# Linear attention with an ELU feed-forward: three uncast first loads, one decayed k, and a written-out order

## The chip, the core and the metric

The kernel runs on one core of a Trainium2 chip. Five engines work side by side, each through its own list of instructions in order: TensorE (PE, matrix products, with its weight loads shown apart as PEld), VectorE (DVE), ScalarE (ACT), GpSimd (POOL) and SyncE (SP). Transfers run on 16 DMA engines. A transfer is issued by SP or ACT on a hardware queue, or by POOL on a software queue; in this kernel a load that turns 32-bit floats into 16-bit ones is issued by POOL. The metric is the device time of one execution in microseconds (us). A kernel's time is the median of several runs.

## The reference

The first part is attention without a softmax, with a decay `lam` per head, in blocks with a running state; the second is a feed-forward layer with ELU.

```python
B, H, S, D = q.shape                      # 4, 8, 768, 64; block = 64
Dmask = np.where(rel >= 0, lam[:, None, None] ** rel[None, :, :], 0.0)
lam_pow = lam[:, None, None] ** (pos[None, :, None] + 1)
for b in range(nb):
    intra = np.einsum('bhic,bhjc->bhij', qb, kb) * Dmask[None]
    intra = np.einsum('bhij,bhjd->bhid', intra, vb)
    inter = np.einsum('bhid,bhde->bhie', qb * lam_pow[None], kv_state)
    out[:, :, sl] = intra + inter
    rev_pow = lam[:, None, None] ** (block - 1 - pos[None, :, None])
    kb_dec = kb * rev_pow[None]
    kv_state = lam_block * kv_state + np.einsum('bhsd,bhse->bhde', kb_dec, vb)
# then, with x of 3072 tokens x 512:
h = x @ w_in                              # 512 x 2048
g = np.where(h > 0.0, h, np.exp(np.minimum(h, 0.0)) - 1.0)
return (g @ w_out).astype(np.float32)     # 2048 x 512
```

## The kernel before

**Tiles.** The kernel takes blocks of 128 positions, not 64, so a sequence has 6 chunks. A *group* g is one chunk of one batch: g // 4 is the chunk and g % 4 the batch, 24 groups in all. A group is 128 tokens by 512 features (8 heads of 64). Groups 0 to 3 are loaded one by one, later ones in pairs. `w_in` and `w_out` are loaded in eight pieces each (`wi16_0` to `7`, `wo16_0` to `7`). Tiles on the chip are 16-bit, the arrays in memory 32-bit.

**Work of a group.** `T`: q and k are transposed, on PE with an identity for groups 0 to 7 (into `psT`, line 283, copied out on DVE to `qT` with a multiply by `qs` in line 290 and on ACT to `kT` in line 291), by DMA transposes on SP's queue for later groups (line 268). `S`: products of k and q into two `psS` (302). `E`: DVE multiplies them by `mask`, which holds causality and a decay (318), into `pp`. `P`: `pp` and v into `psO` (338), and from chunk 1 on the state and q too (344). Then `psO` goes to `xt`, on ACT (359) or, from group 8, on DVE with a multiply by `qs` (361). `kd`: POOL multiplies k by its decay `ks` (174). `U`: kd and v into `psU` (397 as four matmuls, 406 as eight of half width), and DVE adds it to the old state, which POOL has multiplied by `upp` (378), giving the new state `st` (416, 418).

**Feed-forward.** `1:g:j`: 16 matmuls (8 of 256 columns once groups go in pairs) with pieces of wi into `psH` (478), which has two banks; ACT writes `e` = exp (484) and relu in place (485); DVE joins both to `g` (457), which frees the bank. `2:g:j`: four matmuls with pieces of wo into `psM` (499); after four such units the row of the output goes to `osb` (525) and out over SP (450). A unit `1:g:j` with j = 0 needs wi pieces 0 and 1 in groups 0 to 3, j = 1 pieces 2 and 3, and so on; the same holds for `2:g:j` and wo.

**Order.** Every engine works through its instructions as written. POOL's list is `POOL_ORDER` (k0 is a load, i0 a piece of wi, o0 of wo, d0 a multiply `kd`, m4 a state multiply). `OPEN` is the order of all other work up to the first unit of group 8, where w2 and w6 are matmuls on zeros; from there a loop at the end of the function writes the order with the offsets in `AT` and a lag `LAGU` of the `2` units. In front of everything stand ten matmuls on zeros (line 84). `q0` is the one tile that is loaded in 32 bits, on SP's queue (line 117), and cast on DVE (127). `BANKS` says which of the eight PSUM banks each result takes.

Some results of DVE and ACT (`pp`, `xt`, state updates) are kept in a list `late` and issued one at a time between feed-forward units.

Of the kernel before, what the change touches and what calls it, by code (L numbers as in the profile page):

```python
# [7 lines left out]
FP32 = mybir.dt.float32  # L8
# [7 lines left out]
def kernel(  # L16
# [30 lines left out]
    POOL_ORDER = (  # L47
        "k0 k1 iota q1 k2 v1 i0 v0 q2 i1 v2 i2 o0 i3 d0 q3 o1 i4 k3 i5 o2 o3 v3 d1 m4 d2 d3 i7 "
        "o4 o5 i6 o7 k4 o6 q4 m5 k6 v4 q6 k10 q10 d5 d4 d6 m6 v6 k8 q8 v8 d7 m7 v10"
    )  # L50
    RAW = "q0"
    FIRST = "q0:0 c0 c1 c2"
    OPEN = (
        "z1 z0 z3 Z1 Z2 Z0 z2 T0 w2 T1 S0 S1 w6 P0 P1 T2 1:0:0 S2 1:1:0 P2 U0 M 1:2:0 1:0:1 2:0:0 "
        "1:1:1 2:1:0 1:2:1 T3 2:2:0 1:0:2 S3 1:2:2 2:2:1 2:1:1 P3 1:1:2 1:3:0 2:0:1 2:0:2 "
        "2:1:2 1:1:3 U1 1:2:3 M Z3 2:2:2 1:3:2 U2 1:3:1 2:1:3 1:0:3 T5 T4 2:2:3 1:3:3 S4:5 "
        "2:0:3 2:3:2 2:3:0 M U3 M B:P4:P5:U4:U5 W8 2:3:3 1:4:1 T6 W9 1:4:0 T7 2:3:1 1:4:3 S6:7 "
        "1:4:2 2:4:0 2:5:0 1:4:5 1:4:4 2:4:1 B:P6:P7:U6:U7 1:4:7 1:6:1 2:5:2 2:5:1 1:6:0 1:4:6 "
        "2:4:2 S8:9 1:6:2 1:6:3 2:4:3 2:5:3 W11 W10 1:6:4 B:P8:P9:U8:U9 1:6:5 1:6:6 2:6:0 "
        "2:6:1 L12 1:6:7 2:6:2 1:8:0 S10:11 2:6:3 1:8:1 2:7:0 1:8:2 2:7:1"  # L60
    )
    LAGU = 7
    AT = {"L": -18, "W": -13, "T": -9, "S": -8, "B": -4}
    BANKS = (
        "S0=M0,M1 S1=C,D S2=D,M1 S3=D,B P0=M1 P1=B P2=B P3=D U0=M0 U1=D U2=A U3=M1 T0=M1,C "
        "T1=D,A T2=A,D T3=D T4=M0 T5=A T6=M1 T7=D M2=C M3=M0"
# [14 lines left out]
    def zero_matmuls(n):  # L81
# [4 lines left out]
    zero_matmuls(10)  # L86
# [4 lines left out]


# [27 lines left out]
    nc.scalar.preload_act_table_set("natural_log_exp_and_others")  # L120

    def cast_raw(g, w, eng):
        n = f"{w}{g}"
        t = asb.tile([128, 1, H, 64], FP16, tag=f"{w}n1", name=f"{w}n{g}", bufs=4)
        (qg if w == "q" else kg)[g] = t
        if eng == 0:
            nc.vector.tensor_copy(t[:, 0], raw[n][:])
        else:
            nc.scalar.copy(t[:, 0], raw[n][:])

    def of(tiles, g):
        g0, i = group_of[g]
        return tiles[g0][:, i]
# [25 lines left out]

    iota_c = cpool.tile([128, 1], I32, name="iota_c")  # L160
    iota_r = cpool.tile([128, 128], I32, name="iota_r")

    def emit_iota():
        nc.gpsimd.iota(iota_c[:], pattern=[[0, 1]], base=0, channel_multiplier=1)
        nc.gpsimd.iota(iota_r[:], pattern=[[1, 128]], base=0, channel_multiplier=0)

    kds, qkT, Pt, psS, xg = {}, {}, {}, {}, {}

    def att_kd(g):
        if g // B == NCB - 1:  # L170
            return
        kd = asb.tile([128, H, 64], FP16, tag="kd", name=f"kd{g}", bufs=8)
        kds[g] = kd
        nc.gpsimd.tensor_tensor(  # L174
            out=kd[:], in0=of(kg, g),
            in1=ks[:].unsqueeze(2).broadcast_to([128, H, 64]), op=ALU.mult,
        )


    pool_list = POOL_ORDER.split()  # L180

    def emit_pool():
        w = pool_list.pop(0)
        if w == "iota":
            emit_iota()
        elif w[0] in "qkv":
            emit_load(w[0], int(w[1:]))
        else:
            {"i": emit_wi, "o": emit_wo, "d": att_kd, "m": lambda g: att_M(g)}[w[0]](int(w[1:]))

    def emit_pool_run():
        while pool_list and pool_list[0][0] != "m":
            emit_pool()

# [15 lines left out]

    dn = cpool.tile([128, H], FP32, name="dn")
# [451 lines left out]
```

## Time and profile before

| | us |
|---|---|
| runs: median of 3 (lowest, highest) | 215.49 (215.18, 215.7) |
| the profiled execution: span from first to last instruction | 213.2 |
| TensorE busy | 202.7 |
| VectorE, ScalarE busy | 130.1, 129.0 |
| GpSimd busy | 96.2 |
| TensorE busy, 0 to 5 us | 3.81 |
| TensorE busy, 5 to 10 us | 2.95 |
| TensorE busy, 15 to 20 us | 3.88 |
| TensorE busy, 35 to 50 us | 15.0 of 15 |

The span is less than the time of a run; the difference of the median, 2.3 us, lies before the first and after the last instruction. Busy time of TensorE is counted from the start of a matmul to its modelled end; matmuls overlap, so that one of 512 columns lasts some 380 ns in the table but the next starts 216 ns after it. Work on TensorE is therefore counted here by the distance from start to start. The granted clock is 1.00 nearly throughout, though the first ten matmuls on zeros start 0.43 us apart.

A line of the order of time reads: start, duration, engine, line of the kernel, operation, result <- sources, count, and in brackets how long the engine was idle before and what ended that.

### The profile page before, as it was taken

To read this page: it belongs to the slowest core of one execution; us is meant where nothing else is said; L and a number is where in the kernel's file an instruction comes from. 1 tells how busy PE (TensorE), PEld (TensorE's weight loads), DVE (VectorE), ACT (ScalarE), POOL (GpSimd) and SP (SyncE) were. 2 spreads that over 40 slices of the span, in tenths; PEclk is the share of its full clock that TensorE was granted. 3 is DMA by queue.
4 is the path that set the end of the run, shared out by engine and by line. 5 is a ranking of instruction groups with operands and counts; after the bars stand their busy time and mean duration, and the time that the engine had idled before them with its cause. 6 is when DMAs were issued, how large, how long until landed. Compare 5 with 4: busy or idle time off the path is not lost.

```text
span 213.2 us, 5156 instructions
## 1 busy us (share of the span) xinstructions
PE 202.7 (95%) x2066; PEld 138.1 (65%) x2066; DVE 130.1 (61%) x224; ACT 129.0 (61%) x245; POOL 96.2 (45%) x115
## 2 busy tenths in 40 slices
PE   7667999999999999999999999999999999999994
PEld 2355676767686776766766766766766666666652
DVE  3936453777846888677667667667667547533321
ACT  4545654884867756676476476476476576477640
POOL 7996991999972908667166259300000000000000
PEclk9999999999999999999999999999999999999999
DMA  8999999999996999999939919999124110110112
GB/s 90 141 175 193 192 148 173 147 165 147 153 165 145 111 197 107 144 122 116 129 106 125 167 59 103 144 180 161 52 65 83 52 49 0 54 51 16 36 49 98
DMA packets 101976, 24.59 MB, mean 115 GB/s; under 512 B 92608, under 2 KB 99008, under 8 KB 101952
## 3 DMA queue, kind: packets, MB, share of 16 engines
q0 software_dynamic: 79760, 13.50, 83.1%
q1 hardware_dynamic: 22192, 10.76, 24.6%
q8 instruction: 16, 0.26, 0.5%
q14 instruction: 8, 0.07, 0.1%
HBM read 27.27 MB, written 6.29 MB: 157 GB/s over the span
## 4 chain that ended last, share of the span: by engine, by line
PE 82%; POOL 8%; DMA 7%; issue 1%; ACT 1%; DVE 0%; POOLq 0%; ACTq 0%
PE psM L499 36%; PE psH L478 35%; DMA wi<-in_moe_w_in_dram 4%; DMA wo<-in_moe_w_out_dram 3%; PE psO L338 3%; PE psS L302 3%; PE psO L344 2%; POOL kd L174 1%; POOL wi L148 1%; POOL kn L109 1%; POOL vn L109 1%; PE psU L406 1%; PE psT L283 1%; POOL qn L109 1%; POOL wo L155 1%
## 5 line engine op out<-in xcount | busy, mean ns | idle before, releaser
L478 PE MATMUL psH<-xt,wi 128*128 128x256 f16 (+1 forms) x896 | 99.3, 258 | 2.0 <-DMA wi<-in_moe_w_in_dram 1.1
L457 DVE SCALAR_TENSOR_TENSOR g<-e,psH 128x512 f16<-128x512 f32 x96 | 65.8, 686 | 56.7 <-ACT psH L485 56.0
L484 ACT ACTIVATE e<-psH 128x512 f32<-128x512 f32 x96 | 57.3, 597 | 65.0 <-PE psH L478 62.8
L499 PE MATMUL psM<-wo,g 128*128 128x512 f16 (+1 forms) x384 | 95.6, 377 | 0.7 <-DMA wo<-in_moe_w_out_dram 0.7
L478 PEld LDWEIGHTS <-wi 128*128 128x128 f16 x896 | 76.9, 98 | 27.4 <-DMA wi<-in_moe_w_in_dram 1.8
L485 ACT ACTIVATE psH<-psH 128x512 f32<-128x512 f32 x96 | 57.0, 593 | 0.0
L499 PEld LDWEIGHTS <-g 128*128 128x128 f16 x384 | 35.9, 98 | 29.3 <-issue 1.3
L318 DVE TENSOR_TENSOR pp<-psS,mask 128x512 f16<-128x512 f32 x48 | 30.8, 684 | 4.4 <-PE psS L302 4.4
L174 POOL TENSOR_TENSOR kd<-kn,ks 128x512 f16<-128x512 f16 x20 | 20.7, 1040 | 21.3 <-DMA kn<-in_k_dram 20.4
L378 POOL TENSOR_TENSOR stt<-st,upp 64x256 f32<-64x256 f16 x32 | 19.5, 608 | 14.7 <-DVE st L418 8.9
L109 POOL DMA_DIRECT2D vn<-in_v_dram x14 | 15.5, 1108 | 1.7 <-DMA wi<-in_moe_w_in_dram 1.7
L109 POOL DMA_DIRECT2D kn<-in_k_dram x14 | 15.5, 1105 | 0.8 <-POOLq L647 0.8
L525 ACT COPY osb<-psM 128x512 f32<-128x512 f32 x23 | 13.5, 590 | 3.2 <-PE psM L499 3.2
L109 POOL DMA_DIRECT2D qn<-in_q_dram x13 | 14.8, 1138 | 0.0
L418 DVE TENSOR_TENSOR st<-stt,psU 64x256 f16<-64x256 f32 x32 | 13.3, 416 | 1.2 <-PE psU L406 0.5
L361 DVE TENSOR_TENSOR xt<-psO,qs 128x512 f16<-128x512 f32 x16 | 11.0, 688 | 3.5 <-PE psO L344 3.5
L338 PE MATMUL psO<-pp,vn 128*64 128x128 f16 x192 | 12.0, 222 | 1.2 <-DMA vn<-in_v_dram 1.0
L338 PEld LDWEIGHTS <-vn 128*64 128x64 f16 x192 | 9.7, 110 | 4.6 <-issue 2.9
L344 PE MATMUL psO<-qT,st 128*64 128x128 f16 x160 | 10.0, 219 | 0.0
L344 PEld LDWEIGHTS <-st 128*64 128x64 f16 x160 | 8.9, 110 | 0.0
L302 PE MATMUL psS<-qT,kT 64*128 64x128 f16 x192 | 7.9, 218 | 0.3 <-ACT kT L291 0.3
L359 ACT CAST xt<-psO 128x512 f16<-128x512 f32 x8 | 4.4, 588 | 6.4 <-PE psO L338 4.3
(44 smaller groups left out, 72.3 us busy)
## 6 DMA issues: line engine op xcount, KB each, us to landing
out_dram<-osb SPq DMA_DIRECT2D x23, 256.0 KB, 2.2
kn<-in_k_dram POOLq DMA_DIRECT2D x10, 256.0 KB, 7.8
qn<-in_q_dram POOLq DMA_DIRECT2D x10, 256.0 KB, 6.8
vn<-in_v_dram POOLq DMA_DIRECT2D x10, 256.0 KB, 7.6
wi<-in_moe_w_in_dram POOLq DMA_DIRECT2D x8, 256.0 KB, 6.9
wo<-in_moe_w_out_dram POOLq DMA_DIRECT2D x8, 256.0 KB, 7.7
kn<-in_k_dram POOLq DMA_DIRECT2D x4, 128.0 KB, 4.2
vn<-in_v_dram POOLq DMA_DIRECT2D x4, 128.0 KB, 5.5
```

Of the source, the lines that this page charges most:

```text
L109: nc.gpsimd.dma_start(out=t[:].rearrange("p b h d -> p (b h) d"), in_=src)
L174: nc.gpsimd.tensor_tensor(out=kd[:], in0=of(kg, g), in1=ks[:].unsqueeze(2).broadcast_to([128, H, 64]), op=ALU.mult,)
L302: nc.tensor.matmul(psS[g][hh][:, hp, :], lhsT=kt[r, hp, :], rhs=qt[r, hp, :], start=True, stop=True,)
L318: nc.vector.tensor_tensor(out=P[:], in0=pts[hh][:], in1=mask[:, hh::2, :], op=ALU.mult)
L338: nc.tensor.matmul(po[r, hp, :], lhsT=vt[:, 2 * hp + hh, :], rhs=Pt[(g, hh)][:, hp, :], start=True, stop=(cb == 0), skip_group_check=True,)
L344: nc.tensor.matmul(po[r, hp, :], lhsT=st[b][cb % 2][:, hp, r], rhs=qt[:, hp, :], start=False, stop=True, skip_group_check=True,)
L378: nc.gpsimd.tensor_tensor(out=tmp[r], in0=old[r, :, r], in1=upp[r].unsqueeze(2).broadcast_to([64, NHP, 64]), op=ALU.mult,)
L457: nc.vector.scalar_tensor_tensor(out=g[:].rearrange("p f c t -> p (f c t)"), in0=e[:], scalar=-1.0, in1=r[:], op0=ALU.add, op1=ALU.min,)
L478: nc.tensor.matmul(pH[:, f * n * 128 : (f + 1) * n * 128], lhsT=wi16[i][:, kk, w * 128 : (w + 1) * 128], rhs=xg[g0][:, kk, :], start=(kk = ...
L484: nc.scalar.activation(e[:], pH[:], AF.Exp)
L485: nc.scalar.activation(pH[:], pH[:], AF.Relu)
L499: nc.tensor.matmul(psM[g][:, cols], lhsT=gts[(g, j * FB + f)], rhs=wo16[i][:, w, cols], start=first and f == 0, stop=end and f == FB - 1, ...
```

## The change

The change has these parts.

- `RAW` names three tiles that are loaded in 32 bits on hardware queues: q0 and q1 by SP, k0 by ACT. There is no cast: `scaled` multiplies them by a decay and writes 16 bits, k0 and q0 on DVE, q1 on POOL.
- k is multiplied by its decay `ks` = lam^(128 - p) once, and the product `kd` serves both for `psU` and for the transposes, on PE or by DMA. All 24 groups are multiplied now, k0 to k3 and k7 on DVE, the others on POOL. q has the counterpart: `qn` = lam^(p - 128) on the raw tiles, `qs` in the copy of the transposed tile for groups 2 to 7, `qs` on `xt` from group 8 on.
- `mask` is gone; `psS` is multiplied by `causT`, which holds only 0 and 1.
- The state update is turned round: DVE adds `psU` to the state first (`att_Y`), and POOL multiplies the sum by `upp` after that (`att_M`). `psU` of chunk 0 is made by eight matmuls of half width too.
- The eight matmuls on zeros of `w2` and `w6` are gone; the first ten stay.
- `ORDER` writes the order of all work out: loads, constants, multiplies, transposes (`t`) and their copies (`e`), `s`, `E`, `p`, `x` (with an engine: a is ACT, v DVE), `u`, `y`, `m`, `1`, `g` (DVE's join) and `2`. Lists `late`, `pending`, `POOL_ORDER`, `OPEN`, `AT` and the loop at the end are gone. `BANKS` names banks for more results.

```diff
-    POOL_ORDER = (
-        "k0 k1 iota q1 k2 v1 i0 v0 q2 i1 v2 i2 o0 i3 d0 q3 o1 i4 k3 i5 o2 o3 v3 d1 m4 d2 d3 i7 "
-        "o4 o5 i6 o7 k4 o6 q4 m5 k6 v4 q6 k10 q10 d5 d4 d6 m6 v6 k8 q8 v8 d7 m7 v10"
-    )
+    RAW = "q0S k0A q1S"
+    ORDER = (
+        "z:0:1:v i:0 iota row col log z:2:1:v ks a:k0:v L:k1 L:k2 ident L:q2 qn t:k0 z:2:0:a L:v0 a:q0:v "
+        "z:0:0:v t:q0 L:v1 e:q0:a logp e:k0:a upp a:q1:p i:1 i:3 z:1:1:a i:2 d:1:v L:k3 d:2:v L:v2 z:3:0:a "
+        "t:q1 t:k1 e:q1:v e:k1:a caus L:q3 z:3:1:v L:k4 t:k2 qs:2 s:1 i:5 E:1:0 u:0 i:4 t:q2 L:q4 qs:3 L:v3 "
+        "e:k2:a s:0 o:0 z:1:0:a o:1 E:1:1 d:5:p qs:1 E:0:1 d:4:p u:1 i:7 i:6 qs:0 o:5 p:1 x:1:a e:q2:v o:4 "
+        "E:0:0 y:1 y:0 L:v4 L:q6 1:1:0 o:2 s:2 E:2:0 o:3 p:0 g:1:0 x:0:a L:k6 o:7 o:6 1:1:1 E:2:1 L:v8 1:0:0 "
+        "d:3:v p:2 u:2 L:q8 t:k3 e:k3:a t:q3 g:1:1 x:2:a 1:0:1 e:q3:v s:3 g:0:0 y:2 1:2:0 g:0:1 L:k8 t:k5 "
+        "g:2:0 t:k4 e:k4:a 1:0:2 1:1:2 E:3:0 E:3:1 t:q5 g:0:2 t:q4 p:3 d:6:p u:3 e:k5:a g:1:2 1:2:1 e:q4:v "
+        "x:3:v 1:2:2 g:2:1 y:3 2:0:0 g:2:2 1:3:0 2:1:0 e:q5:v 1:0:3 L:v6 s:5 s:4 g:3:0 E:5:0 g:0:3 E:5:1 "
...
+    )
-    FIRST = "q0:0 c0 c1 c2"
-    OPEN = (
-        "z1 z0 z3 Z1 Z2 Z0 z2 T0 w2 T1 S0 S1 w6 P0 P1 T2 1:0:0 S2 1:1:0 P2 U0 M 1:2:0 1:0:1 2:0:0 "
-        "1:1:1 2:1:0 1:2:1 T3 2:2:0 1:0:2 S3 1:2:2 2:2:1 2:1:1 P3 1:1:2 1:3:0 2:0:1 2:0:2 "
...
-    )
...
+    for w in RAW.split():
+        g0 = int(w[1:-1])
+        raw[w[:-1]] = asb.tile([128, H, 64], FP32, name=f"raw_{w[:-1]}", tag=f"raw_{w[:-1]}")
+        {"S": nc.sync, "A": nc.scalar}[w[-1]].dma_start(
+            out=raw[w[:-1]][:], in_=xin[w[0]][g0, :, 0:L].rearrange("h p d -> p h d")
+        )
...
+    def scaled(w, g, eng):
+        t = asb.tile([128, H, 64], FP16, tag="kd" if w == "k" else "qd", name=f"{w}d{g}", bufs=8 if w == "k" else 4)
+        {"v": nc.vector, "p": nc.gpsimd}[eng].tensor_tensor(
+            out=t[:], in0=raw[f"{w}{g}"][:],
+            in1=(ks if w == "k" else qn)[:].unsqueeze(2).broadcast_to([128, H, 64]), op=ALU.mult,
+        )
...
+    def att_T_dma(w, g):
+        t = asb.tile([128, NHP, 128], FP16, tag=f"{w}T", name=f"{w}T{g}", bufs=6)
+        src = of("q", g) if w == "q" else kds[g][:]
+        nc.sync.dma_start_transpose(out=t[:], in_=src.rearrange("p h d -> p (h d)"))
+        qkT[(w, g)] = t
...
+    def att_E(g, hh):
+        P = asb.tile([128, NHP, 128], FP16, tag="pp", name=f"pp{g}_{hh}", bufs=6)
+        nc.vector.tensor_tensor(
+            out=P[:], in0=psS[g][hh][:],
+            in1=causT[:].unsqueeze(1).broadcast_to([128, NHP, 128]), op=ALU.mult,
+        )
...
     def att_M(g):
...
-            nc.gpsimd.tensor_tensor(
-                out=tmp[r], in0=old[r, :, r],
+            nc.gpsimd.tensor_tensor(
+                out=new[r, :, r], in0=stt.pop((g, hh))[r],
                 in1=upp[r].unsqueeze(2).broadcast_to([64, NHP, 64]), op=ALU.mult,
             )
+    def att_Y(g, hh):
...
+            nc.vector.tensor_tensor(
+                out=tmp[r], in0=stp[b][cb % 2][r, :, r], in1=src, op=ALU.add
+            )
```

## The prediction

> **What bounds the kernel now.** I read the page's forty slices first, then the engines' busy time by stage, then the order of time up to 81 us with what each TensorE wait was for.
>
> ```profile
> PE   7667999999999999999999999999999999999994
> POOL 7996991999972908667166259300000000000000
> DMA  8999999999996999999939919999124110110112
> GB/s 90 141 175 193 192 148 173 147 165 147 153 165 145 111 197 107 144 122 116 129 106 125 167 59 103 144 180 161 52 65 83 52 49 0 54 51 16 36 49 98
> ```
>
> TensorE (PE) is full from about slice 5 to the last; only the opening, where the DMA engines and GpSimd (POOL) are full instead, has room.
>
> ```profile
> 5.00:10.00 5.00, 2.95 (x37) 1.67 (x37) 4.90 (x10) 3.32 (x11) 5.00 (x7) 1.00 1.86 138
> 10.00:15.00 5.00, 3.37 (x48) 2.19 (x47) 2.15 (x4) 1.63 (x3) 4.93 (x7) 1.00 1.91 170
> 20.00:25.00 5.00, 4.18 (x49) 3.07 (x50) 1.80 (x3) 2.36 (x5) 4.13 (x6) 1.00 1.56 192
> 50.00:60.00 10.00, 10.00 (x109) 7.27 (x102) 8.02 (x14) 6.57 (x14) 9.64 (x11) 1.00 2.29 150
> ```
>
> The columns are the stretch, its length, then busy us of PE, PE's weight loads, VectorE (DVE), ScalarE (ACT) and POOL. ACT and DVE are half idle while PE waits. The order of time names what PE waits for:
>
> ```profile
> 7.95 0.40 PE L283 MATMUL psT<-ident,qn 128*128 128x128 f16 x4 [1.31 <-DMA qn<-in_q_dram]
> 12.07 0.64 PE L338 MATMUL psO<-pp,vn 128*64 128x128 f16 x16 [1.03 <-DMA vn<-in_v_dram]
> 14.38 0.62 PE L478 MATMUL psH<-xt,wi 128*128 128x128 f16 x8 [0.40 <-DMA wi<-in_moe_w_in_dram]
> 20.46 0.62 PE L478 MATMUL psH<-xt,wi 128*128 128x128 f16 x8 [0.66 <-DMA wi<-in_moe_w_in_dram]
> 21.88 0.38 PE L499 MATMUL psM<-wo,g 128*128 128x512 f16 x1 [0.36 <-DMA wo<-in_moe_w_out_dram]
> 34.26 1.46 PE L499 MATMUL psM<-wo,g 128*128 128x512 f16 x6 [0.35 <-DMA wo<-in_moe_w_out_dram]
> 35.59 0.90 PEld L478 LDWEIGHTS <-wi 128*128 128x128 f16 x16 [0.37 <-DMA wi<-in_moe_w_in_dram]
> 80.33 1.04 PE L478 MATMUL psH<-xt,wi 128*128 128x256 f16 x8
> ```
>
> Until 36 us a landing load ends nearly every PE wait. The last line is psH 8:0, where I compare: from there to the end both programs hold the same matmuls in the same order, and ahead of it the same list of work.
>
> **That list in PE time.** Spacings from the order of time: a psH unit 0.87 us, a psM unit 0.865, transposes of one group 0.45, its psS 0.28, its psO 0.25 in chunk 0 and 0.44 later, psU 0.22 as four matmuls, 0.175 as eight of half width. Ahead of 8:0 stand 8 groups of transposes (3.6), 10 of psS (2.8), 4 + 6 of psO (3.6), psU (2.0), 32 psH (27.9) and 27 psM (23.4): 63.3 us. It starts at 80.33, so 17.0 us are lost. The change can only win from these.
>
> **How loads land now.** Call 256 KB of f32 read one unit: a q, k or v tile of one group; a pair's tile or a piece of wi or wo is two. In issue order the waits above give landings: 4 units (q1) at 7.9, 9 (v0) at 12.05, 12 (wi1) at 14.4, 19 (wi3) at 20.4, 22 (wo1) at 21.9, 38 (wo5) at 34.2, 40 (wi6) at 35.6. A transpose that waited for q2 (10 units) began at 12.9. The line through 10 and 40 is 30 / 22.7 = 1.32 units per us, and 22 lies on it: from 13 us on bandwidth rules. Before that POOL's issue does: 0.91 us for a tile of one group, 0.80 for a wi piece, with about 3.5 us from issue end to landing (q1: 4.39 to 7.9).
>
> **Part 1, hardware queues.** q1 and k0 leave POOL (2 x 0.91 us), and wi0 goes first. POOL now issues wi0 until 2.05, the iotas to 2.5 (two, 0.16 and 0.26), then k1, k2, q2, v0, v1, five times 0.91, until 7.0; then the multiply of q1. SP and ACT issue three f32 tiles (0.4 us each, as raw q0 at 1.19) meanwhile. ACT's table load (1.28) moves behind its one issue to 2.4, and nothing needs it before lam at 3.6. At issue end + 3.7 us v1, the tenth unit, lands at 10.7 where the tenth now lands at 12.9. wi1 is issued by 8.9, lands at 12.4 (14.4 now); after wi3 and wi2 16 units are there at 15.4, and the line of 1.32 goes on from that point: v2 16.9, q3 17.7, k4 19.2, wi5 and wi4 20.7 and 22.2, v3 24.5, wo0 and wo1 26.0 and 27.5, wi6 30.6, wo4 (40 units) 33.6. That is **2.0 us ahead** of 35.6. A load also waits until the eighth ahead of it has landed (v3's issue sat 1.7 us until wi3 was there); by these times no issue is late for that, nor for POOL's wait for k4. Three f32 tiles at once appear in no row; nearest is raw q0, 3.3 us beside POOL's first loads, so k0 lands at 4 to 4.5 and q1 at 5 to 6.5. The lead is bounded by 0 (the shared rate eats it) and 2.7 (three tiles off POOL at 0.91); I take 2.0 as the layout gives it.
>
> **Part 2, decay multiplied once.** q1's multiply on POOL reads f32; the row for f16 is 1.04 us, for f32 sources 0.608 at half the elements (stt), so 1.0 to 1.3. I take 1.04. In front of it wait qn (ACT, after lam at 3.6) and raw q1; behind it in POOL's queue wi1, wi3, wi2 and every later load, so each us it is late is a us off the lead. DVE gets k0, q0, k1, k2, k3, k7 (six at 0.68) and loses the decay mask (1.20), the cast of raw q0 (0.67); two qT multiplies become copies of like size, and DVE takes kT of 6 and 7 and xt of 3, 4, 5 and 7 over from ACT (six at about 0.65, late enough to lie in its idle half). DVE's chain: k0 at 4.35 to 5.05, ident 0.51, q0 to 6.3, k1 (landed 7.1) to 7.8, k2 to 8.7, qT1 9.4, causT and a memset to 10.05, both halves of psS 1 to 11.4; psO at 11.45, ACT's xt 0.58, psH 1:0 at 12.3 against 13.37 for the first psH now. Later k tiles keep the count of POOL's 1.04 us multiplies but feed the DMA transposes now: kd 1.04, issue 1.25, landing up to 3.7, 6.0 in all, under the 8 or more us of matmuls that the order puts between kd and psS. Should that cover be gone, a pair costs up to 2 us, eight pairs. The state's multiply (POOL, 2 x 0.608) moves behind DVE's add; its reader is four groups on, some 30 us, so nothing.
>
> **Part 3, mask and psU.** causT broadcast over heads reads as the mask did: 0.684 us by that row. psU of chunk 0 saves 4 x 0.045 = 0.2 us of PE.
>
> **Part 4, zero matmuls.** The eight behind the first ten (0.59 + 1.47 us) fall in waits; removing them gains nothing beyond that. The ten run 0.43 us apart, the later six about 0.22, so PE starts at half speed though the rows grant a clock of 1.00. [...]
>
> **Part 5, the order.** Laid out by these landings: psH 1:0 at 12.3 to 13.2, psS 2 and psO 0, then a wait for wi2 to 15.4; 1:1 and 0:0 to 17.2; psO 2, psU 2, transposes of 3 to 18.2; 0:1, psS 3, 2:0 to 20.9; transposes of 5 and 4, the second behind POOL's kd4 (k4 issue chain, two at 1.04 from 19.7) at 21.8; 0:2 at 22.2 with wi4; 1:2, 2:1, 2:2 to 27.1; psM 0:0 with wo1 at 27.5; 3:0, psM 1:0; 0:3 with wi6 at 30.6; psS 5, 4 and 3:1 to 33.0; psM 1:2 with wo4 at 33.6. Done by then: transposes 2.7, psS 1.7, psO 1.0, psU 0.7, 12 psH 10.5, 2 psM 1.7, together 18.3 of 63.1. From there 44.8 us of work: 78.4 without a stop. Now, from 35.6 (19.8 done, 43.5 left, 79.1 without a stop) 8:0 comes 1.2 us later, in pipeline drains and waits for DVE's g (0.47 twice, 0.2). With 0.2 to 1.2 of that kind 8:0 starts at 78.6 to 79.6; middle 79.1, **1.2 us earlier**. The span goes from 213.2 to 212.0; 2.3 us lie around it (215.49 less 213.2), so the runs go to 214.3.
>
> **Rivals.** *ACT and the two psH banks become the bound; slower.* The new order puts eight psH units (1:1 to 2:2) before the first psM. A unit holds its bank for 0.87 + 0.17 drain + 0.60 + 0.59 + 0.69, about 3.0 us, so two banks pass one per 1.5: eight take 12.0 of the 12.1 us from 15.4 to 27.5. Between 15.4 and 33.6 ACT has 11.5 x 1.19 + 4 x 0.585 = 16.0 of 18.2 us, DVE 15.3. It decides once fixed order puts more than 0.4 us of other work (kT, xt, state) in that loop's way. With four such blocks of 0.6 to 0.7 us 8:0 comes 2.5 us later than laid out: 216.8. For: now psM units alternate with psH and hide the loop. Against: ACT's idle there now.
> *The lead is eaten.* The f32 tiles share the rate, or q1's multiply holds POOL; 2.0 us go to 0.8 or less: 215.5. For: DMA slices are full from the second on. Against: 138 GB/s from 5 to 10 us, 192 later, so early bandwidth is free.
> *Half clock.* psH 1:1 and 0:0 each 0.87 us longer, of which waits at 20 to 22 us hide 0.9: 0.8 later, 215.1. Only the first ten matmuls speak for it.
> *All drains close.* Lead 2.7 and the waits at 20 to 31 us shrink: gain 3.2, 212.3. For: PE idles 5.6 us after 13.4 now. Against: the loop above is full.
>
> **Numbers.** Forecast (0.5 to 2.4 us won) 0.48; all close 0.12; lead eaten 0.08 and half clock 0.06, both within 0.2% or about 0.43 us, what runs of this kernel can tell; slower 0.26. So faster 0.60, same 0.14, slower 0.26. The likeliest's own range is 213.1 to 215.0. The whole reaches down to the gain of 3.2 and a little more, 211.9, and up past 216.8 to 217.2, leaving out about 0.15.
>
> **What would show it.** Right: raw k0, q1 landed before 6.5, POOL's multiply of q1 near 7, v1 by 11, wi2 by 15.5, wo4 by 33.6, psH 8:0 at 79.1, and the same 133 us behind it. Wrong: wi1 later than 13.5; PE waits between 16 and 33 us released by ACT or DVE g and not by DMA; matmuls of 128 columns 107 ns apart after 9 us; psS of groups 8 and up waiting for kT.

## The result, and the profile after

The change made the kernel slower. The runs after it have a median of 218.23 us (217.54 to 218.84), those of the kernel before beside them 215.34 (215.03 to 215.7): a ratio of 1.0137, with a 95% interval of 1.0102 to 1.0172. The profiled execution has a span of 215.8 us against 213.2. psH 8:0, the point of comparison, starts at 83.00 us against 80.33, 2.67 later, which is the whole difference of the spans (2.6). Behind it both take the same 132.8 us. The profiled execution was the fastest of the four, so the medians differ by a little more (2.9). All times here and below are of the chip's faster state; one of the ten executions of e6 below (220.23 us) was in a slower one and is left out.

The forty slices of the kernel after, as shown of before:

```profile
PE   7189989999999999999999999999999999999994
POOL 7598796463879500028373382383383200000000
PEclk9755999999999999999999999999999999999999
DMA  4999999999999913409979769769679620110112
```

PE is nearly empty in the second slice (5.4 to 10.8 us), and its granted clock is half in the third and fourth. The stages of the opening, with the columns as above:

```profile
5.00:10.00 5.00, 1.10 (x10) 0.53 (x8) 2.07 (x7) 2.10 (x7) 2.33 (x4) 0.83 1.75 192
10.00:15.00 5.00, 4.20 (x54) 2.82 (x56) 4.24 (x8) 2.55 (x7) 5.00 (x7) 0.50 1.79 149
15.00:20.00 5.00, 3.83 (x45) 3.06 (x42) 4.65 (x10) 2.26 (x4) 4.35 (x5) 0.50 1.66 141
```

PE's order of time, with what ended its idle time:

```profile
10.73 0.60 PE L286 MATMUL psTq<-ident,qd 128*128 128x128 f16 x4 [3.20 <-POOL qd L245]
16.06 1.87 PE L433 MATMUL psH<-xt,wi 128*128 128x128 f16 x16 [0.68 <-ACT xt L358]
19.53 3.09 PE L433 MATMUL psH<-xt,wi 128*128 128x128 f16 x32 [0.49 <-DMA wi<-in_moe_w_in_dram]
28.12 1.05 PE L433 MATMUL psH<-xt,wi 128*128 128x128 f16 x16 [0.56 <-DVE g L418]
32.02 1.03 PE L453 MATMUL psM<-wo,g 128*128 128x512 f16 x4
83.00 1.04 PE L433 MATMUL psH<-xt,wi 128*128 128x256 f16 x8
```

The first unit psH 1:0 takes 1.87 us where a unit at full speed shows 1.05 (the fourth line); the next two take 3.09 together. The longest wait is for POOL's multiply of q1, and POOL's own order of time tells why:

```profile
9.63 1.04 POOL L245 TENSOR_TENSOR qd<-raw_q,qn 128x512 f16<-128x512 f32 x1 [2.67 <-DMA raw_q<-in_q_dram]
10.62 2.31 POOL L167 DMA_DIRECT2D wi<-in_moe_w_in_dram  x3
```

POOL had issued v1 by 6.96, stood 2.67 us until raw q1 was there, multiplied it, and only then issued wi1, wi3 and wi2. The chain of waits up to 20 us (start, duration, what) runs through exactly these:

```profile
1.66 7.82 DMA raw_q<-in_q_dram
...
9.63 1.04 POOL qd L245
10.67 1.49 POOL wi L167 x2
12.17 7.32 DMA wi<-in_moe_w_in_dram
...
19.53 3.09 PE psH L433 x32
```

Raw q1 took 7.8 us from its issue to its landing. It stood behind raw q0 on SP's own queue, which landed at 6.29 (4.53 in the kernel before). The DMA packets show how the queues shared the engines. First the kernel before, from 2 to 6 and from 6 to 10 us:

```profile
DMA packets 3465, 0.56 MB, mean 139 GB/s; under 512 B 3465, under 2 KB 3465, under 8 KB 3465
DMA packets 3312, 0.56 MB, mean 141 GB/s; under 512 B 2935, under 2 KB 3312, under 8 KB 3312
```

The kernel after, in the same two stretches, with the queues of the first:

```profile
DMA packets 2396, 0.62 MB, mean 156 GB/s; under 512 B 2212, under 2 KB 2396, under 8 KB 2396
q1 hardware_dynamic: 1172, 0.27, 30.8%
q10 hardware_dynamic: 1040, 0.26, 29.0%
q0 software_dynamic: 184, 0.09, 18.5%
DMA packets 3797, 0.73 MB, mean 184 GB/s; under 512 B 3469, under 2 KB 3797, under 8 KB 3797
```

A q, k or v tile of one group is 1,040 packets whether it is cast or not, and a raw one writes twice the bytes: ACT's q10 moved only k0, in 1,040 packets and 0.26 MB, and POOL's queue, without k0 and q1, moved 2,080 packets and 0.26 MB less than in the kernel before (77,680 and 13.24 MB against 79,760 and 13.50). So more bytes moved, but from 2 to 10 us 6,193 packets against 6,777 before. The whole shortfall lies before 6 us: while the two hardware queues moved a tile each, POOL's queue moved 184.

What counts is when reads land. From about 9 us on they do so at an even pace in both kernels: a tile of one group some 0.85 us after the read before it, a piece of wi 1.3 to 1.5 us, with half the packets (by the issue records 512 of 512 bytes against 1,024 of 128) and twice the bytes. So neither packets nor bytes alone set this pace. Counted in the prediction's units, the tenth lands at 13.32 us in after and at 12.87 in the kernel before, although POOL ended its issue at 6.96 instead of 8.66. Profiles of like openings differ by about 1 us in this, so it shows that nothing was won, not that something was lost.

### The profile page after: what moved, and what is told of

Its sections match the earlier page's. It is cut to its first block, busy times and chain, and to the rows that moved or that the text cites. A ratio compares the mean times of both kernels' runs of the same rounds, so it can differ in the third digit from the quotient of the medians.

```text
span 215.8 us, 5161 instructions
## 1 busy us (share of the span) xinstructions
PE 204.5 (95%) x2074; PEld 140.8 (65%) x2074; DVE 134.1 (62%) x232; ACT 126.8 (59%) x240; POOL 94.7 (44%) x113
## 3 DMA queue, kind: packets, MB, share of 16 engines
q0 software_dynamic: 77680, 13.24, 81.9%
q10 hardware_dynamic: 1040, 0.26, 0.5%
HBM read 27.27 MB, written 6.29 MB: 156 GB/s over the span
## 4 chain that ended last, share of the span: by engine, by line
PE 82%; DMA 10%; POOL 3%; DVE 2%; ACT 1%; issue 0%; SPq 0%; ACTq 0%; POOLq 0%
PE psM L453 36%; PE psH L433 36%; DMA raw_q<-in_q_dram 4%; DMA kT<-kd 3%; DMA wi<-in_moe_w_in_dram 3%; PE psO L331 3%; PE psS L310 2%; PE psO L337 2%; DVE g L418 1%; PE psU L401 1%; POOL wi L167 1%; POOL stp L368 1%; PE psTq L286 1%; ACT e L439 1%; POOL kn L148 1%; POOL qd L245 0%
## 5 line engine op out<-in xcount | busy, mean ns | idle before, releaser
L433 PE MATMUL psH<-xt,wi 128*128 128x256 f16 (+1 forms) x896 | 101.5, 261 | 2.2 <-DVE g L418 1.0
L433 PEld LDWEIGHTS <-wi 128*128 128x128 f16 x896 | 79.0, 100 | 27.7 <-issue 2.3
L368 POOL TENSOR_TENSOR stp<-stt,upp 64x256 f16<-64x256 f32 x32 | 19.5, 610 | 37.1 <-DVE stt L384 35.3
L317 DVE TENSOR_TENSOR pp<-psS,causT 128x512 f16<-128x512 f32 x48 | 31.2, 685 | 5.7 <-PE psS L310 5.7
L257 POOL TENSOR_TENSOR kd<-kn,ks 128x512 f16<-128x512 f16 x19 | 19.4, 1041 | 29.1 <-issue 16.7
L148 POOL DMA_DIRECT2D qn<-in_q_dram x12 | 13.7, 1143 | 0.8 <-DMA vn<-in_v_dram 0.5
L384 DVE TENSOR_TENSOR stt<-stp,psU 64x256 f32<-64x256 f16 x32 | 13.3, 415 | 0.5
L337 PE MATMUL psO<-qT,stp 128*64 128x128 f16 x160 | 10.3, 219 | 0.0
L337 PEld LDWEIGHTS <-stp 128*64 128x64 f16 x160 | 9.0, 110 | 0.0
L310 PEld LDWEIGHTS <-kT 64*128 64x128 f16 x192 | 5.7, 98 | 3.1 <-issue 2.3
```

Source lines behind the costliest of these rows:

```text
L257: {"v": nc.vector, "p": nc.gpsimd}[eng].tensor_tensor(out=kd[:], in0=of("k", g), in1=ks[:].unsqueeze(2).broadcast_to([128, H, 64]), op=ALU ...
L310: nc.tensor.matmul(psS[g][hh][:, hp, :], lhsT=kt[r, hp, :], rhs=qt[r, hp, :], start=True, stop=True,)
L317: nc.vector.tensor_tensor(out=P[:], in0=psS[g][hh][:], in1=causT[:].unsqueeze(1).broadcast_to([128, NHP, 128]), op=ALU.mult,)
L337: nc.tensor.matmul(po[r, hp, :], lhsT=stp[b][cb % 2][:, hp, r], rhs=qt[:, hp, :], start=False, stop=True, skip_group_check=True,)
L368: nc.gpsimd.tensor_tensor(out=new[r, :, r], in0=stt.pop((g, hh))[r], in1=upp[r].unsqueeze(2).broadcast_to([64, NHP, 64]), op=ALU.mult,)
L433: nc.tensor.matmul(pH[:, f * n * 128 : (f + 1) * n * 128], lhsT=wi16[i][:, kk, w * 128 : (w + 1) * 128], rhs=xg[g0][:, kk, :], start=(kk = ...
```

## The experiments

Times are medians of the runs; the ratio is to the kernel before on the same chip, with its 95% interval. "psH 8:0" and "kT" come from one profiled execution each: the start of that unit, and how long psS of group 9 waited at 62 to 65 us for its transposed k, with waits below 0.2 us given as 0. In the expectations (and in "q of chunk 1") "chunk" n is what the text above calls group n. In the diffs `w:n` is n matmuls on zeros.

| kernel | us | ratio | psH 8:0 | kT |
|---|---|---|---|---|
| after | 218.23 | 1.0137 (1.0102 to 1.0172) | 83.00 | 0 |
| e1_q1_on_dve | 216.40 | 1.0084 (1.0053 to 1.0116) | 81.34 | 0 |
| e2_zeros_back | 217.45 | 1.0129 (1.0104 to 1.0154) | 81.27 | 0.47 |
| e3_before_no_zeros | 215.16 | 1.0014 (0.9992 to 1.0036) | 80.33 | - |
| e4_before_raw3 | 215.40 | 1.0031 (1.0011 to 1.0051) | 81.57 | - |
| e5_q1_dve_warm | 216.34 | 1.0055 (1.0033 to 1.0077) | 81.52 | 0.56 |
| e6_soft_loads | 216.70 | 1.0086 (1.0053 to 1.0120) | 81.89 | 0.8 |
| e7_before_zeros16 | 215.09 | 0.9988 (0.9957 to 1.0019) | 80.34 | - |
| e8_soft_warm | 217.38 | 1.0086 (1.0053 to 1.0119) | 82.70 | 1.2 |
| e9_psm_early | 218.54 | 1.0173 (1.0130 to 1.0215) | 83.66 | 0 |
| e10_psm_early_only | 220.15 | 1.0248 (1.0202 to 1.0293) | 85.83 | 0 |
| e11_g_first | 216.90 | 1.0081 (1.0053 to 1.0109) | 82.36 | 1.35 |
| e12_g_first_p1_early | 216.45 | 1.0067 (1.0041 to 1.0094) | 81.92 | 0.90 |
| e13_k10_all | 215.08 | 1.0001 (0.9983 to 1.0019) | 80.72 | 0 |
| e14_k10_warm | 215.20 | 1.0019 (1.0000 to 1.0037) | 80.66 | 0 |
| e15_k10_only | 217.59 | 1.0110 (1.0071 to 1.0148) | 83.26 | 0.38 |
| e16_s3_later | 215.16 | 1.0011 (0.9990 to 1.0032) | 80.87 | 0 |
| e17_q2_later | 216.32 | 1.0041 (1.0016 to 1.0065) | 82.18 | 0 |

**POOL's wait, and the clock.** e1 takes q1's multiply from POOL; e2 fills PE's gaps with zeros as the kernel before did.

```diff
# e1, ORDER
- upp a:q1:p i:1 i:3
+ upp a:q1:v i:1 i:3
# e2, ORDER
- t:q0 L:v1
+ t:q0 w:14 L:v1
- p:1 x:1:a
+ p:1 w:3 x:1:a
```

> The changed kernel with the multiply of raw q1 on DVE instead of POOL, nothing else. Theory A (the late tile holds POOL's queue: wi1, wi3 and wi2 were issued from 10.62 us, 3.6 us after v1, because the multiply in front of them waited 2.67 us for raw q1): wi1 is issued at about 7.0, the wait for wi2 that ended at 19.5 ends by 17.0, and psH 8:0 comes 1.5 to 2.5 us earlier than 83.0; ratio to the kernel before 1.002 to 1.007. Theory B (the half clock from 8.3 to 22 us is the whole loss): the clock still falls, psH 1:1 and 0:0 still take 1.5 us each, gain below 0.7 us; ratio above 1.010. Theory C (bandwidth rules, an earlier issue lands no earlier): wi2 still at 19, ratio above 1.010.

> The changed kernel with 14 matmuls on zeros behind the transposes of q0 and 3 behind psO of group 1. Theory B (half clock): the granted clock stays at 1.00 from 8 to 22 us, matmuls of 128 columns start 54 ns apart, psH 1:1 and 0:0 take 1.8 us together instead of 3.0, and 1.0 to 2.0 us of the 2.6 come back; ratio 1.004 to 1.009. Theory A (the held queue is the whole loss): the clock is full but PE waits the longer for wi2 and behind it, gain below 0.6 us; ratio above 1.010.

e1 gains 1.66 us at psH 8:0 (by the ratios, 0.5% or 1.1 us; its profiled execution was the fastest of four). POOL issues the three pieces of wi in one go at 6.90, while q1 lands no earlier. PE still ran at half speed:

```profile
6.90 2.28 POOL L167 DMA_DIRECT2D wi<-in_moe_w_in_dram  x3
```

```profile
10.02 0.61 PE L286 MATMUL psTq<-ident,qd 128*128 128x128 f16 x4 [2.33 <-DVE qd L245]
15.42 1.87 PE L433 MATMUL psH<-xt,wi 128*128 128x128 f16 x16 [0.68 <-ACT xt L358]
```

e2's median gains nothing that can be told from the kernel after. Its profiled execution was the fastest of five (215.81; the others 217.05 to 217.69), and the only one known to have run the opening at full speed: there psH 1:0 starts at 14.43 and takes 1.05 us, and PE waits 1.40 us for wi, until 17.71. The two losses overlap: when PE is faster, it waits longer for the read that POOL held back (1.40 us here, 0.49 in after).

The kernel before was asked the same questions from its side: no zeros behind the first ten, three raw tiles, more zeros at the start.

```diff
# e3, OPEN
-  T0 w2 T1 S0 S1 w6 P0 P1
+  T0 T1 S0 S1 P0 P1
# e4
-  POOL_ORDER "k0 k1 iota q1 k2 ..."   RAW = "q0"   FIRST = "q0:0 ..."   OPEN "... w2 T1 ..."
+  POOL_ORDER "k1 iota k2 ..."   RAW = "q0 q1 k0"   FIRST = "q0:0 k0:1 ..."   OPEN "... w2 q1:0 T1 ..."
# e7
-    zero_matmuls(10)
+    zero_matmuls(16)
```

> The kernel before without its eight matmuls on zeros behind the first ten (w2 and w6). Theory B: the clock falls to half somewhere between 8 and 13 us and comes back only in a full stretch, ratio 1.003 to 1.010. If the old order is full enough without them, the clock stays 1.00 and the ratio is 0.998 to 1.002.

> The kernel before with k0 and q1 loaded uncast on the hardware queues too and cast on ACT and DVE, POOL's list shorter by both, all else as before: part 1 alone. The prediction's reading (early bandwidth is free, POOL's issue rules): wi1 lands 1 to 2 us before 14.4 and the ratio is 0.991 to 0.997. The other reading (three 32-bit tiles share the engines with the first software loads, as q1's landing 7.8 us after its issue suggests): q1 lands at 8.5 to 10 instead of 7.9, psO of groups 0 and 1 come later than 12.07 or alike, ratio 0.998 to 1.008.

> The kernel before with 16 instead of 10 matmuls on zeros at the start. With ten at 0.43 us, 4.3 us in all, TensorE is at full speed behind them in some executions and not in others (the matmuls at 5.6 us of the two kernels differ in that). If 16 make it sure and the clock matters in the old order, the lower end of the runs becomes the rule: ratio 0.995 to 0.999. If the loads set the opening there: 0.998 to 1.003.

e3: the clock is half from 9.3 to 16 us (granted 0.50 from 10 to 16), and psH 1:0 starts at 14.98 us against 13.37, in part because v landed 1.1 us later. Yet both stand at the same place at 35.6 us, and psH 8:0 stays at 80.33. The kernel before waits for wi and wo four times before that (0.40, 0.66, 0.36 and 0.35 us), and e3 comes late enough not to. e7 is level too. So in the kernel before the half clock costs nothing, because the reads hold PE up behind it. e4 is the first part of the change alone. It brings no gain: the ratio is 1.0031, and the tenth unit lands at 13.10 us. Later it does have a lead (wi6 lands at 34.41, 1.1 us sooner than before), which shows in no time. In its profiled execution, one of the two slowest of ten, raw q1 is cast at 9.84, psO of groups 0 and 1 starts at 15.41 (12.07 before), and PE ran at half speed until some 16 us (the transposes of one tile take 0.61 us at 10.48 and at 16.40, not 0.40), so its 81.57 can't be laid to the loads alone.

**Both mended, and another way of loading.** e5 joins e1 with warm gaps. e6 and e8 read only q0 raw, the rest by POOL (e8 with e5's zeros).

```diff
# e5, on e1
-    ZEROS = 10
+    ZEROS = 16
# ORDER: w:10 behind t:q0, w:3 behind u:0 and behind p:1
# e6, on after
-    RAW = "q0S k0A q1S"
+    RAW = "q0S"
# ORDER: "L:k0 L:k1 iota L:q1" in front, d:0:v for a:k0:v, no a:q1:p, qs:0 to qs:3 sooner
```

> The changed kernel with both mended: raw q1 multiplied on DVE, and PE kept busy (16 instead of 10 matmuls on zeros at the start, 10 behind the transposes of q0, 3 behind psU 0 and 3 behind psO 1). If the held queue and the half clock are the whole loss beside the missing lead (theory A plus B), the two gains add: matmuls of 128 columns start 54 ns apart from 7 us on, psH 1:1 starts before 17.5, psH 8:0 before 80.6, ratio 0.997 to 1.003. If they overlap (theory D: once one is mended the order behind it, the two psH banks and the late weights, sets psH 8:0), it stays near the 81.3 of each alone and the ratio is 1.005 to 1.009.

> The changed kernel with part 1 undone: k0 and q1 on POOL's software queue again in the order k0, k1, q1, wi0, k2, q2, v0, v1, q1 scaled in the copy of its transpose, the rest as changed (POOL's wi1, wi3, wi2 directly behind v1). If the hardware loads are the loss: q1 lands near 8, psH 1:0 starts before 15, gain of 1.5 to 2.5 us, ratio 1.002 to 1.007, also with the clock at half. If the order behind 16 us is the loss: gain below 0.7 us, ratio above 1.010.

> Software loads of k0 and q1 as in the run before last and the matmuls on zeros of the q1-on-DVE-and-warm run together. If clock and loads are independent and the new order is as good as the old: ratio 0.995 to 1.000. If the new order itself (weights behind the pairs of q and k, psH units one behind the other) costs about 1 us: 1.003 to 1.007, with PE waits for DVE g or wi between 16 and 33 us.

None of the three comes within 1.1 us of 80.33. In e6 and e8, with POOL's reads as before, the tenth unit lands no sooner either (13.36 and 13.67). e5 runs at full speed, and its order of time shows a wait at 62.73 that is only 0.3 us long in the kernel after:

```profile
12.97 0.32 PE L401 MATMUL psU<-vn,kd 128*64 128x64 f16 x8 [0.26 <-DMA vn<-in_v_dram]
15.74 1.05 PE L433 MATMUL psH<-xt,wi 128*128 128x128 f16 x16
62.73 0.40 PE L310 MATMUL psS<-qT,kT 64*128 64x128 f16 x8 [0.56 <-DMA kT<-kd]
81.52 1.04 PE L433 MATMUL psH<-xt,wi 128*128 128x256 f16 x8
```

Its meaning was seen only later. First the loop of the two psH banks was tried.

**The loop of psH.** From psH 1:1 to the first psM the new order holds eight psH units and takes 11.6 to 12.7 us in after and in all versions so far (19.53 to 32.02 in after), as the prediction's slower rival had it. e9 and e10 put two psM units between them, which needs wo sooner.

```diff
# e9 on e5, e10 on after, ORDER
- L:q3 z:3:1:v L:k4 t:k2 qs:2 s:1 i:5
+ L:q3 z:3:1:v o:0 t:k2 qs:2 s:1 o:1
- s:3 g:0:0 y:2 1:2:0 g:0:1 L:k8 t:k5 g:2:0 t:k4 e:k4:a 1:0:2 1:1:2
+ g:0:0 y:2 2:1:0 s:3 1:2:0 g:0:1 L:k8 2:0:0 g:2:0 1:0:2 E:3:0 E:3:1 1:1:2 g:0:2 t:k5 t:k4
...
```

> The changed kernel with the two mends of e5_q1_dve_warm (q of chunk 1 scaled on DVE; 16 zeros at the start and 16 more in the gaps), and an order in which wo's first two pieces are read right behind q3 and two psM units (2:1:0 and 2:0:0) stand between the last psH units of the opening, the transposes of chunks 5 and 4 moving behind. Loop theory (from psH 1:1 to the first psM the two banks of psH let a unit through every 1.5 us, eight units 12.0 us, whatever comes before them): PE's idle time in that stretch, some 2.7 of 12.2 us, is filled by the two psM units, psH 8:0 comes at 79.5 to 80.5 (81.52 without the new order), and the ratio to before is 0.996 to 1.001. Load theory (the transfers of the opening set the pace, and the loop only shows it): psH 8:0 stays at about 81.3 or later, ratio 1.004 to 1.008.

> The changed kernel with the new order of e9_psm_early alone: q of chunk 1 stays on POOL and the ten zeros stay. Loop theory: the late start of psH 1:1 (19.53) stays, but two psM units go into the loop's gaps: 1 to 2 us gained on the changed kernel, psH 8:0 at 81.0 to 82.0, ratio to before 1.004 to 1.009. Load theory: nothing gained, psH 8:0 at about 83, ratio 1.012 to 1.014.

Both theories missed: both kernels are slower. The edit was not clean. With wo and two more pieces of wi ahead of k4 in POOL's list, POOL's multiplies of k5 and k4 came at 27.29 instead of 22.17, and PE waited for them:

```profile
28.39 0.40 PE L287 MATMUL psTk<-ident,kd 128*128 128x128 f16 x4 [0.66 <-POOL kd L258]
29.39 0.40 PE L287 MATMUL psTk<-ident,kd 128*128 128x128 f16 x4 [0.60 <-POOL kd L258]
```

So e9 and e10 say nothing on the loop, only that a read put first makes another late. The stage table of e5 pointed to DVE:

```profile
15.00:20.00 5.00, 4.03 (x63) 2.98 (x60) 4.91 (x10) 3.26 (x6) 3.70 (x6) 1.00 2.18 167
```

DVE is busy 4.91 of 5 us (3.42 in the kernel before), and the waits for g in e5 sum to 1.3 us. e11 lets DVE's g go ahead of other DVE work; e12 also brings psO of group 1 sooner.

```diff
# e11 on e5, ORDER
- s:2 E:2:0 o:3 p:0 g:1:0 x:0:a
+ s:2 o:3 p:0 g:1:0 E:2:0 x:0:a
- 1:0:0 d:3:v p:2 u:2 L:q8 t:k3 e:k3:a t:q3 g:1:1 x:2:a 1:0:1 e:q3:v s:3 g:0:0 y:2 1:2:0
+ 1:0:0 p:2 u:2 L:q8 t:q3 g:1:1 d:3:v x:2:a 1:0:1 t:k3 e:k3:a g:0:0 e:q3:v y:2 1:2:0 s:3
# e12 on e11: E:1:1 ahead of u:0; p:1 x:1:a ahead of d:4:p u:1; qs:1 qs:0 behind x:1; z:1:0 moved, no w:3 behind u:0
```

> e5_q1_dve_warm with three things moved back on DVE's queue in the opening, nothing else: the mask's multiply of chunk 2 (pp) behind the first g, k with decay of chunk 3 behind the second g, the copy of q^T of chunk 3 behind the third; chunk 3's transposes of k and its scores move behind on PE to suit. DVE theory (DVE, 4.91 of 5 us busy from 15 to 20, is what is late in the two-bank loop: the g that frees a bank of psH stands behind some 0.7 us of other DVE work each time): the first psH units of the loop close up, psH 0:0 at 18.9 to 19.1 (19.58), 0:1 at 20.8 to 21.0 (21.50), psH 8:0 at 80.5 to 81.0 (81.52), ratio to before 1.001 to 1.004. Rival (the start sets the end: the first unit comes at 15.74 where before has it at 13.37, and what is behind adds nothing): psH 8:0 stays at 81.3 to 81.6, ratio 1.005 to 1.007.

> e11_g_first with chunk 1's psO and cast moved ahead of chunk 0's state product, its zeros and two of ACT's constants, so that the first psH unit comes sooner after v0's landing (six of the gap's zeros go from between). DVE theory: the unit 1:0 at 15.0 to 15.2 (15.74), but what is gained there is mostly lost again in the loop: psH 8:0 0.2 us or less before e11_g_first's. Start theory (what the first units gain goes through to the end): psH 8:0 0.5 to 0.7 us before e11_g_first's, at 80.0 to 80.4 if both hold, ratio to before 0.998 to 1.002.

The waits for g go in e11 (psH 0:0 and the unit ahead of it run without a gap from 17.93), and in e12 psH 1:0 starts at 15.14. Yet psH 8:0 is later than in e5, at 82.36 and 81.92, and what grew is the wait for kT: 1.35 and 0.90 us. While that wait stands, these runs can't tell what the loop costs.

**The second bound.** What the wait at 62.73 us rests on is seen in e5's order of time for POOL and for SP's queue, and in its chain of waits (the last line: start, duration, what):

```profile
50.58 2.04 POOL L257 TENSOR_TENSOR kd<-kn,ks 128x512 f16<-128x512 f16 x2 [4.22 <-DMA kn<-in_k_dram]
52.57 1.21 POOL L148 DMA_DIRECT2D kn<-in_k_dram  x1
55.06 1.21 POOL L148 DMA_DIRECT2D vn<-in_v_dram  x1
...
51.64 1.19 SPq L279 DMA_TRANSPOSE kT<-kd  x1
52.93 1.22 SPq L279 DMA_TRANSPOSE qT<-qn  x1
54.20 1.63 SPq L412 DMA_DIRECT2D out_dram<-osb  x2
55.92 4.92 SPq L279 DMA_TRANSPOSE kT<-kd  x2
...
55.92 6.76 DMA kT<-kd
```

POOL stands 4.2 us until k of groups 8 and 9 is there, and has both multiplied by 52.62. SP then issues the transposes of k and q of group 8, two stores of output, and at 55.92 the transpose of k of group 9. That lands 6.76 us later, at 62.68, and psS of group 9 starts at 62.73. However soon PE comes there, it waits. Meanwhile POOL issued two reads: k of groups 10 and 11 at 52.57 and v of 12 and 13 at 55.06. The read of v lands at 62.72, at the same time as the transpose. In after, e1, e2, e5, e6, e8, e11 and e12 these two land within 0.2 us of each other (64.17 and 64.16 in after). Why the transpose ends with the read is not shown. (The expectations of e13 and e15 speak of chunk 11, but its transposes serve work at 82 us; the wait is group 9's.) In the kernel before psS of group 8 stands only at 68.83, some 7 us later than in e5 (61.77), and there the transpose is in time. e13 to e15 issue the read of k of 10 and 11 ahead of the two multiplies, in the 4.2 us that POOL stands.

```diff
# e14 on e5, e15 on after, e13 on e12 (there also qs:1 qs:0 ahead of p:1 again), ORDER
- L:q10 d:8:p g:2:3 d:9:p D:q9 2:1:1 L:k10 g:3:2
+ L:q10 L:k10 d:8:p g:2:3 d:9:p D:q9 2:1:1 g:3:2
```

> e12_g_first_p1_early with two things moved: the read of k of chunks 10 and 11 is issued by POOL ahead of the decay multiplies of chunks 8 and 9 (which wait 4.2 us for their own k, with that issue behind them), and two constants of ACT stand ahead of the cast again, not behind. Second-bound theory (every mended version stops at 62.5 to 63.6 us on the transposes by DMA of k with decay of chunk 11, which wait for a read that POOL issued late): the wait of psS for kT (0.90 in e12) is gone, the two waits of psS behind the first unit (0.53 and 0.37) too, psH 8:0 at 79.8 to 80.6 (81.92), ratio to before 0.996 to 1.001. Rival (the load stream as a whole is late, so that k of chunk 10 sooner makes another tile late): psH 8:0 at 81.0 or later, ratio 1.003 or more.

> e5_q1_dve_warm with the one read moved as in e13_k10_all. Second-bound theory: psS's wait for kT (0.56) goes and nothing else changes, psH 8:0 at 80.9 to 81.0 (81.52), ratio to before 1.001 to 1.004. Rival (load stream): 81.4 or later, 1.005 to 1.008.

> The changed kernel with the one read moved, nothing else. Second-bound theory: there PE comes to psS of chunk 11 at 63.7 us and finds kT there, so nothing is gained: psH 8:0 at 82.8 to 83.1 (83.00), ratio to before 1.012 to 1.015. Rival (late reads cost the changed kernel itself): psH 8:0 at 82.5 or earlier, ratio under 1.011.

POOL and then PE in e14:

```profile
46.23 1.16 POOL L149 DMA_DIRECT2D kn<-in_k_dram  x1
50.52 2.04 POOL L258 TENSOR_TENSOR kd<-kn,ks 128x512 f16<-128x512 f16 x2 [3.13 <-DMA kn<-in_k_dram]
```

```profile
61.64 0.62 PE L311 MATMUL psS<-qT,kT 64*128 64x128 f16 x16
80.66 1.04 PE L434 MATMUL psH<-xt,wi 128*128 128x256 f16 x8
```

The read of k is issued 6.3 us sooner (46.23 against 52.57) and that of v, behind the multiplies, 1.3 us sooner (53.76). The transpose of group 9, issued at 55.83 as in e5, lands at 61.39: 5.6 us on, not 6.8. psS waits no more, and psH 8:0 is 0.86 sooner than in e5; e13 is 1.20 sooner than e12. Whether k out of the way or v sooner did it is not shown. In e15, where the opening is late, the same edit gives no gain at psH 8:0 (83.26, where 82.8 to 83.1 was expected), and kT is not there in time as expected: the pair of psS of groups 8 and 9 takes 1.11 us there and 0.85 in after, against 0.56 without a wait. Its ratio, 1.0110, can't be told from 1.0137.

So of the 83.00 us of after, the hold of POOL and the half clock together were worth 1.48 (e5) and this one read 0.86 more (e14, at 80.66). The kernel before stands at 80.33, and both e13 and e14 are level with it. e13 and e14 also settle what e11 and e12 left open: they differ by those edits, neither waits for kT, and psH 8:0 is at 80.72 and 80.66. Waits for g in the loop of psH did not set it.

**Is anything left in the new order?** e16 removes a wait that e11's order had made, e17 also reads q2 behind wi.

```diff
# e16 on e13, ORDER
- 1:2:0 s:3 g:0:1 L:k8 t:k5 g:2:0 t:k4 e:k4:a
+ 1:2:0 g:0:1 L:k8 t:k5 g:2:0 t:k4 s:3 e:k4:a
# e17 on e16: L:q2 behind i:2; t:q2 e:q2:v s:2 E:2:0 E:2:1 behind 1:1:1
```

> e13_k10_all with chunk 3's scores moved behind the transposes of chunks 5 and 4 on PE, nothing else: they waited 0.64 for the copy of k^T on ACT, and 0.9 us of transposes can run in that time. If PE is the bound from there on (the traces of e13 show it busy in all but 0.5 us from 25 to 80): psH 8:0 at 80.1 to 80.3 (80.72), ratio to before 0.996 to 0.999. If the reads set the pace again: the wait turns up again at a vn, wi or kT, psH 8:0 at 80.6 or later, ratio 0.999 to 1.003.

> e16_s3_later with the read of q of chunk 2 issued behind the first four pieces of wi instead of ahead of v, and chunk 2's transpose of q, its scores and products moved behind the second psH unit. The opening's first waits in e13 are for reads (wi 0.67 at 17.2, vn 0.26 and 0.40, qn 0.30). If the packets of the tiles ahead set when wi lands (q of chunk 2 is 1024 of them, about 1.1 us at 950 a microsecond): wi's wait goes, psH 1:1 at 16.0 to 16.4 (17.16), psH 8:0 0.4 to 1.0 us before e16's, ratio to before 0.992 to 0.997. If not, or if q of chunk 2 is then what is waited for: no better than e16.

Neither beats the kernel before. e13 shows what its opening waits for now:

```profile
14.56 1.06 PE L434 MATMUL psH<-xt,wi 128*128 128x128 f16 x16
17.16 1.96 PE L434 MATMUL psH<-xt,wi 128*128 128x128 f16 x32 [0.67 <-DMA wi<-in_moe_w_in_dram]
19.52 0.41 PE L332 MATMUL psO<-pp,vn 128*64 128x128 f16 x8 [0.40 <-DMA vn<-in_v_dram]
```

Reads again: wi2 is waited for until 17.16 us, where the prediction had it at 15.4, and from there to the first psM (29.57) it takes 12.4 us, about the 12.1 laid out. e13's psH 8:0 comes 1.6 us behind the 79.1 of the prediction, about as much as wi2 is late. In e16 the wait of psS for a copy turned into waits for POOL's kd (1.1 us). In e17 wi's wait went, though wi2 landed only 0.2 us sooner (16.85), and PE waited 0.93 us for the copy of q2 on DVE. That execution ran at half speed from 13 to 17 us (psS took 0.59 us at 13.16 and 0.40 at 20.24, psH 1:0 took 1.87 at 15.88); its clock is 0.992 on average, as in seven others (215.57 to 216.74), while four at 1.00 took 215.21 to 215.38, level with the kernel before. No version was found that is faster than the kernel before, and a version with both mends and an earlier stream of reads was not tried.

## Why the prediction was wrong

**The step that failed** is the landing times of part 1. The prediction held that before 13 us POOL's issue sets the pace: "At issue end + 3.7 us v1, the tenth unit, lands at 10.7", and with it came the lead of "2.0 us ahead" from which psH 8:0 at 79.1 was laid out. POOL's issue did end early, at 6.96, but the tenth unit landed at 13.32, and somewhere from 12.8 to 14.1 in every version of the new order, as in the old opening (12.9 to 14.0 in the kernel before, e3, e4 and e7). The reads were landing one after another at their even pace by then, so a read that is issued sooner mostly stays longer under way: from the end of its issue the tenth unit took 6.36 us in after, and 4.21 in the kernel before. In the kernel before that distance grew over POOL's first nine reads already, from 2.99 us (k0) to 4.92 (wi1), so 3.7 was no constant. Nor did the raw tiles come as given: with two more of them in flight k0 landed at 5.44 instead of 4 to 4.5, and q1, behind q0 on one queue, at 9.48 instead of 5 to 6.5. The lead at the fortieth unit (wo4), 33.6 against 35.6, became 36.70, about 1.1 us behind; with POOL's hold mended it is 35.29 in e5 and 35.22 in e13, a lead of some 0.3. The note "early bandwidth is free" (138 GB/s against 192 later) failed with it.

**"Each us it is late is a us off the lead"** held. POOL's multiply was put near 7 and started at 9.63; wi1 to wi2 were issued at 10.6 to 12.9, and wi2 landed at 19.48 instead of 15.4. Moving this multiply to DVE (e1) brought wi2 in at 17.14 and took 1.66 of the 2.67 us back. The rival "the lead is eaten" named both mechanisms, "the f32 tiles share the rate, or q1's multiply holds POOL", but was priced as the loss of the lead alone, 215.5. The loss of the lead is no floor: what waits in POOL's list goes below zero.

**The half clock** was priced at 0.8 us and 215.1, with psH 1:1 and 0:0 each 0.87 us longer. That the clock would fall again behind the start was the author's estimate; the trace of the kernel before does not show it. It came, with the sign the prediction named: the matmuls of psH 1:0 in after start 106 to 107 ns apart, those of psH 0:1, at 23.48 us, 55 to 56. psH 1:0 takes 1.87 us, 0.82 longer than at full speed, and 1:1 and 0:0 together 3.09 against 1.96 in e13, 1.1 longer where the rival had 1.7, since the distance drops to 56 ns within 0:0. The granted clock is half between about 8.3 and 22 us (0.50 from 9 to 21.5). What brings it down is not shown: in after it falls 3.0 us behind the last of the ten zeros, which ends at 5.33, but only 0.8 us behind transposes, which end at 7.53, and in e3 it falls at 9.3 with no PE wait above 1.3 us ahead of it. What the cases missed is that it and the hold of POOL occur together and cover each other, so their prices don't add: zeros alone (e2) can't be told from no change, q1 on DVE alone (e1) gives 0.5%, and e5 with both lies within e1's interval.

**Part 2, "6.0 in all, under the 8 or more us of matmuls"**, cost about 0.3 us in the changed kernel, and so little only because the opening was late: in the six mended versions e2, e5, e6, e8, e11 and e12 psS of group 9 waits 0.47 to 1.35 us for it. The cover was there (10.6 us in e5, from the start of the multiply to PE's arrival), but from there to the landing it took 11.1 us, not 6.0. The multiply took its 1.04. Then 3.3 us passed until SP issued the transpose, behind group 8's transposes and two stores, and the landing came 6.76 us behind the issue, not 1.25 and up to 3.7. (In the kernel before 3.7 is the median for q's transposes from issue to landing; they took 2.4 to 7.5, k's 2.4 to 7.9.) The prediction's own sign, "psS of groups 8 and up waiting for kT", is what showed it.

**The rival with the right sign** had the wrong reason. It gave 216.8 by the two psH banks, with eight units at 1.5 us. The eight units do take some 12 us, but PE is busy in most of that time (waits for g are 0.8 us in after and 1.3 in e5), and taking the waits for g away gained nothing at psH 8:0, neither while the second bound stood (e11) nor without it (e13 against e14).

**What held.** The loss lies ahead of psH 8:0 alone (2.67 us there, 2.6 in the span, the same 132.8 behind); the mask, psU and the state's multiply brought PE no wait above 0.3 us in after. The range ended at 217.2 and the time is 218.23: it was bounded by one mechanism at a time, and here the lost lead, the hold of POOL and the half clock came together.

## What to carry to other kernels

Before paying for an earlier issue, list when the reads land. Here they landed at an even pace while the distance from issue to landing grew, and issuing the tenth unit 1.7 us sooner (6.96 against 8.66) landed it no sooner (13.32 against 12.87). A multiply on the engine that issues the reads is a wait for every read behind it (2.67 us here, in front of three pieces of wi); put the issue ahead of whatever may wait. When a mend gains less than its wait was long, look for the wait that grew: here a second one, 45 us further on, took 0.5 of the 2.0 us that e5 had won at the first psM (30.04 against 32.02), until one issue was moved. The tool's chain names what it infers; who issued what, and when it landed, has to be read from the queues.

## What was not expected of the hardware

- Raw q1 on SP's hardware queue took 7.8 us from issue to landing, behind raw q0 there and beside ACT's tile and POOL's reads, and POOL's queue moved 184 of 2,396 packets from 2 to 6 us.
- Tiles of one group land some 0.85 us apart and pieces of wi 1.3 to 1.5, though a piece has half the packets and twice the bytes.
- The granted clock isn't a sure sign at the start: in e1 it reads 1.00 until 20 us, while its transposes took 0.61 us instead of 0.40 and its first psH unit 1.87 instead of 1.05.
- Whether the ten zeros (some 4.3 us) bring full speed differs between executions of like kernels: in after the transposes at 6.48 take 0.38 us, in e1, with the same ten, those at 6.42 take 0.58.
